# Decode attention over a 65,536-key cache: V loaded 8 MB at a time, and the first weight load in one piece

## The chip, the cores and the metric

The kernel runs on one core of a Trainium2 chip; the other cores are idle. The metric is device time in microseconds. The kernel before takes 1292.25 us (median of 3 runs, 1292.07 to 1292.52).

## What is computed

One token is decoded: layer norm, then attention with 16 query heads over 8 key/value heads, each with 65,536 cached keys and values of 256 bf16 elements, plus a small gated feed-forward part. The reference, cut to what matters:

```python
x  = A_x                                   # [1, 1, 448]
xn = _layernorm(x)
# attention: Hq = 16, Hkv = 8, Sk = 65536, Dh = 256, all bf16
q  = (xn @ wq)                             # wq: [448, 4096], 3.67 MB
k, v = repeat(k_cache, 2), repeat(v_cache, 2)   # each cache: 268 MB
p  = softmax(q k^T * Dh**-0.5)
a  = (p v) @ wo                            # wo: [4096, 448]
# the other part (w_gate, w_up, w_down: 448 x 1792 each, 1.6 MB)
y  = (silu(xn @ w_gate) * (xn @ w_up)) @ w_down * sigmoid(xn @ w_r)
out = x + a + xn + y
```

Nearly all of it is reading: K and V together are 537 MB, and every byte is used once (for the two query heads of its group).

## The kernel before

K and V go through a ring of 4 slots in SBUF. A slot is 128 partitions x 32 KB (4 MB): 64 keys or values of 256 bf16 for each partition. A head has 512 keys for each partition, so 4 turns (`U`) of 2 slots (`HC`).

```python
NSLOT = 4          # ring slots
CH = 64            # keys of one partition in a slot
HC = 2             # slots of K (or V) in a turn
LAST = [32, 16, 8, 8]
...
ring = S_("ring", [P, NSLOT * SLOT], BF16)          # SLOT = CH * Dh
```

All loads of the stream are issued by SyncE, in program order. A slot is filled again only when TensorE is through with the load that lay in it (`FREE`):

```python
def slot_item(kd, u, c, parts=None):
    src = A_k_cache if kd == "k" else A_v_cache
    h, n0 = u // U, (u % U) * SBN + c * CH
    r = rounds[0]
    rounds[0] += 1
    s = r % NSLOT
    ...
    for k, (sem, J) in enumerate(parts or [("slot%d" % s, CH)]):
        ap = ring[:, s * SLOT + o * Dh:s * SLOT + (o + J) * Dh]
        item((kd, u, c, k), [(ap.rearrange("p (j d) -> p j d", d=Dh),
                              src[0, h].rearrange("(p n) d -> p n d", p=P)[:, n0 + o:n0 + o + J, :], sem)],
             [("FREE", r - NSLOT)] if r >= NSLOT and k == 0 else ())
```

The order of the loads: wq in two parts; the K of the first head (8 slots, with the weights of the other part amid them); then 28 turns of K, V, V, K, in which the K are those of the next head; then 4 turns of V alone. The last slot of the ring is, in those 4 turns, cut in four parts (32, 16, 8 and 8 keys), so that TensorE can begin on it early.

```python
item("wq", [(w_area[o:e, 0:WQN], flat_src(A_wq, WQN)[o:e, :], "wq") for o, e in ((0, P // 8), (P // 8, P))])
for u in range(U):
    for c in range(HC):
        slot_item("k", u, c)
    if u == U // 2 - 1:
        item("wg", ...)      # w_gate, w_up: after the query is there
        item("wd_a", ...)
for t in range(NT):          # NT = 28
    slot_item("k", t + U, 0)
    slot_item("v", t, 0)
    slot_item("v", t, 1)
    if t % U == 0:
        item(("wo", t // U), ..., [("ATTN", t - 1)] if t else ())
    slot_item("k", t + U, 1)
for t in range(NT, NU):      # NU = 32
    for c in range(HC):
        slot_item("v", t, c, last_parts(rounds[0]) if rounds[0] % NSLOT == NSLOT - 1 else None)
```

`flat_src` views wq as 128 rows of 14,336 elements (28 KB), one for each partition.

TensorE's order in one of the 28 turns: it transposes and uses the first K slot (`k_slots`), multiplies the weights of the softmax with the first V slot (`pe_V`), sums the weights, uses the second V slot, then the second K slot. A V slot is waited for by its own semaphore and free when its last matmul is done:

```python
def turn_B(t):
    ...
    k_slots(sets_of(u, 0), s0, at)
    pe_V(t, 0, True, True)
    pe_tot(t)
    pe_V(t, 1, True, True)
    dve_ob(t)
    k_slots(sets_of(u, 1), s0, at)
    ...

def pe_V(t, c, first, last, loose=False):
    ...
    r, got = items[("v", t, c)]
    for k, (key, ap, o0, J) in enumerate(got):
        W_item("pe", key)
        ...
    alias("pe", "FREE", r)
```

At the end TensorE waits for the second half of w_down and for the last rows of wo, which are the last loads of the stream, and a short chain on TensorE and VectorE makes the result.

Of the kernel before, what the change touches and what calls it, by code (L numbers as in the profile page):

```python
# [11 lines left out]
NSLOT = 4  # L12
CH = 64
# [6 lines left out]
def bass_parallel_sum__gqa_block_cached__moe_arch_mod__decode_kernel(  # L20
# [17 lines left out]
    P = 128  # L38
    _, Hkv, Sk, Dh = A_k_cache.shape
# [16 lines left out]
    SBN = HC * CH  # L56
    SETS = SBN // SETN
    U = NPP // SBN
    NT = U * (Hkv - 1)
# [8 lines left out]
    SLOT = CH * Dh  # L68
    WQN, WGN, WDN, WON = RP * HqDh // 2, RP * F, FH * D, rep * NH * D
# [4 lines left out]
    def S_(name, shape, dtype):  # L74
        t = nc.sbuf_tensor(name, shape, dtype)
        sb.append(t)
        return t.__enter__()

    ring = S_("ring", [P, NSLOT * SLOT], BF16)
    w_area = S_("w_area", [P, WQN], BF16)  # L80
# [85 lines left out]
    def W(e, *key):  # L166
        prog[e].append(("w", here[0], key, None, None))
# [12 lines left out]
    items = {}  # L180
    semtot = {}
    rounds = [0]

    def item(key, parts, need=()):
        for n in need:
            W("sp", *n)
        for ap, src, sem in parts:
            semtot[sem] = semtot.get(sem, 0) + 16
            items[key] = (sem, semtot[sem])
            prog["sp"].append(("d", here[0], ("DMA", key, len(prog["sp"])), (ap, src), sem))  # L190

    def slot_item(kd, u, c, parts=None):
        src = A_k_cache if kd == "k" else A_v_cache
        h, n0 = u // U, (u % U) * SBN + c * CH
# [3 lines that stand above are left out]
        o = 0  # L198
        got = []
# [5 lines that stand above are left out]
            got.append(((kd, u, c, k), ap, o, J))  # L205
            o += J
        items[(kd, u, c)] = (r, got)

    def flat_src(src, n):
        return src.rearrange("a b -> (a b)").rearrange("(p n) -> p n", p=P)  # L210

    def wo_src(h):
        return A_wo[h * rep * Dh:(h + 1) * rep * Dh, :].rearrange("(i p f) n -> p i f n", i=rep, f=NH)

    def wo_view(t):
        return t.rearrange("p (i f n) -> p i f n", i=rep, f=NH)
# [4 lines left out]
    def last_parts(r):  # L221
        return [("last%d" % k if k < len(LAST) - 1 else "slot%d" % (r % NSLOT), J) for k, J in enumerate(LAST)]

    item("wq", [(w_area[o:e, 0:WQN], flat_src(A_wq, WQN)[o:e, :], "wq") for o, e in ((0, P // 8), (P // 8, P))])
    for u in range(U):
        for c in range(HC):
            slot_item("k", u, c)
        if u == U // 2 - 1:
            item("wg", [(w_area[:, 0:WGN // 2], flat_src(B_w_gate, F), "wg"),
                        (w_area[:, WGN // 2:WGN], flat_src(B_w_up, F), "wg")], [("QT",)])  # L230
            item("wd_a", [(wd_a[:, :], wd_src(0), "wd")])
    for t in range(NT):
        slot_item("k", t + U, 0)
        slot_item("v", t, 0)
        slot_item("v", t, 1)
        if t % U == 0:
            item(("wo", t // U), [(wo_view(wo_cur[:, :]), wo_src(t // U), "wo")], [("ATTN", t - 1)] if t else ())
        slot_item("k", t + U, 1)
    for t in range(NT, NU):
        for c in range(HC):  # L240
            slot_item("v", t, c, last_parts(rounds[0]) if rounds[0] % NSLOT == NSLOT - 1 else None)
    item("wd_b", [(w_area[:, 0:WDN], wd_src(1), "we0")], [("FFN1",)])
# [661 lines left out]
```

## Time and profile before

| | before |
|---|---|
| time, median of 3 | 1292.25 us |
| span of the profiled run | 1290.7 us |
| bytes moved | 549.22 MB, mean 426 GB/s |
| TensorE matmul busy | 926.4 us (72%) |
| VectorE busy | 586.1 us (45%) |
| ScalarE busy | 459.5 us (36%) |
| first K slot used by TensorE | 30.14 us |
| result leaves | 1289.19 us |

How to read the views: the page gives, for 40 equal slices of the span, the busy share of each engine in tenths and what the DMA engines moved in GB/s; a list of DMA issues with the size of each and the median time from issue to landing; and the chain that ended last, followed back from the last instruction. The timeline lists instructions in order of time: start and duration in us, engine, source line, operation, output<-input, count, and in brackets the idle time ahead of it and what ended it (`<-DMA ring` is a load into the ring). SPq is the queue of SyncE, which issues the loads; several issues with waits between them are merged in one line. In the table by stage, a line has the stretch, its length, the busy time of TensorE (matmuls, weight loads), VectorE, ScalarE and GpSimd with their counts, the clock granted to TensorE, the share of the 16 DMA engines that was busy, and GB/s; a packet's bytes are counted where it starts. A packet record is one descriptor's transfer by one DMA engine.

### The profile page before, as it was taken

Reading aid. Unit: us, or ns where it says so; the run is one execution under the profiler, and the core shown is the slowest. Engines: PE = TensorE matmul, PEld = TensorE weight load, DVE = VectorE, ACT = ScalarE, POOL = GpSimd, SP = SyncE. Lnnn points to the kernel's source line nnn. Section 1 sums busy time; section 2 is a strip of 40 time slices with the busy share of each in tenths; the row PEclk is TensorE's granted clock in tenths of the full one; section 3 lists DMA queues with packets and bytes.
Section 4 is the critical chain, followed back from the end, with each engine's and each line's share of the span. In section 5 each row is a group of like instructions: output and inputs, shape, how many; then the busy total and the mean of one; then the engine's idle time right before and its main releaser. Section 6 shows DMA issues by size and latency. Waiting matters only on the chain.

```text
span 1290.7 us, 22879 instructions
## 1 busy us (share of the span) xinstructions
PE 926.4 (72%) x9824; PEld 671.7 (52%) x9824; DVE 586.1 (45%) x1091; ACT 459.5 (36%) x655; POOL 4.6 (0%) x35
## 2 busy tenths in 40 slices
PE   1988776876767866768766668766678766678654
PEld 1867554654545654545645546545456544456421
DVE  2756444553445544445544445544345434455300
ACT  1545433442323533334433244333334333334300
POOL 1000000000000000000000000000000000000000
PEclk9989889988889888889878899888798888898876
DMA  9999999999999999999999999999999999999997
GB/s 307 423 434 434 429 432 433 428 437 429 432 434 429 435 431 432 433 431 434 431 432 432 431 434 431 433 432 431 434 430 434 432 430 435 430 434 432 430 431 317
DMA packets 22244, 549.22 MB, mean 426 GB/s; under 512 B 2387, under 2 KB 4438, under 8 KB 5206
## 3 DMA queue, kind: packets, MB, share of 16 engines
q1 hardware_dynamic: 22226, 549.04, 99.6%
q8 instruction: 8, 0.13, 0.0%
q14 instruction: 6, 0.05, 0.0%
q10 hardware_dynamic: 4, 0.00, 0.0%
HBM read 549.03 MB, written 0.00 MB: 425 GB/s over the span
## 4 chain that ended last, share of the span: by engine, by line
DMA 68%; PE 31%; SPq 0%; ACT 0%; issue 0%; DVE 0%
DMA ring<-in_A_k_cache_dram 63%; PE ps_t L352 24%; PE ps_q L352 5%; DMA w_area<-in_B_w_down_dram 3%; DMA ring<-in_A_v_cache_dram 2%; PE ps_s L352 1%; PE ps_m L352 1%; SPq L776 0%; ACT s L430 0%; DVE res_bf L727 0%; PE ps_o L352 0%
## 5 line engine op out<-in xcount | busy, mean ns | idle before, releaser
L352 PE MATMUL ps_t<-ident_f,ring 128*128 128x128 f32 x4096 | 568.7, 296 | 248.3 <-DMA ring<-in_A_k_cache_dram 229.2
L406 DVE COPY kt_buf<-ps_t 128x1024 bf16<-128x1024 bf16 x768 | 489.8, 683 | 427.0 <-PE ps_t L352 426.7
L352 PEld LDWEIGHTS ps_t<-ident_f,ring 128*128 128x128 f32 x4096 | 494.9, 152 | 354.3 <-DMA ring<-in_A_k_cache_dram 245.6
L408 ACT ACTIVATE kt_buf<-ps_t 128x1024 bf16<-128x1024 bf16 x256 | 262.1, 1024 | 357.9 <-PE ps_t L352 357.8
L430 ACT ACTIVATE s<-ps_q 98x512 bf16<-98x512 f32 x256 | 152.9, 597 | 288.0 <-PE ps_q L352 288.0
L352 PE MATMUL ps_o<-ring,p_sb 128*4 128x512 bf16 x2048 | 134.0, 404 | 67.5 <-DMA ring<-in_A_v_cache_dram 67.5
L352 PE MATMUL ps_q<-kt_buf,q_cur 128*2 128x512 bf16 x2048 | 166.4, 402 | 0.0
L352 PEld LDWEIGHTS ps_o<-ring,p_sb 128*4 128x4 bf16 x2048 | 48.0, 86 | 134.4 <-issue 77.6
L352 PEld LDWEIGHTS ps_s<-sel_bf,s 128*128 128x128 bf16 x1024 | 60.6, 99 | 54.1 <-ACT s L430 50.8
L540 DVE CAST ob_sb<-ps_o 100x512 bf16<-100x512 f32 x29 | 20.1, 692 | 144.5 <-PE ps_o L352 144.5
L352 PE MATMUL ps_s<-sel_bf,s 128*128 128x8 bf16 x1024 | 64.3, 168 | 22.6 <-ACT s L430 22.6
L497 ACT ACTIVATE p_sb<-S_sb 128x128 bf16<-128x128 bf16 x64 | 18.9, 307 | 136.1 <-PE ps_o L352 135.8
L576 DVE TENSOR_TENSOR rowsf<-ps_m,rowsf 1x448 f32<-1x448 f32 x28 | 17.1, 612 | 54.1 <-PE ps_m L352 54.1
L352 PEld LDWEIGHTS ps_q<-kt_buf,q_cur 128*2 128x2 bf16 x2048 | 27.1, 80 | 10.2 <-issue 5.0
L512 DVE RECIPROCAL rs<-ps_m 128x4 f32<-128x4 f32 x29 | 5.3, 182 | 52.8 <-PE ps_m L352 52.8
L352 PE MATMUL ps_m<-wo_cur,oT_sb 128*1 128x448 bf16 x112 | 25.8, 352 | 0.0
L352 PEld LDWEIGHTS ps_m<-rowsum,ones_f 128*128 128x128 f32 x116 | 15.1, 190 | 12.6 <-issue 12.6
L352 PE MATMUL ps_m<-rowsum,ones_f 128*128 128x2 f32 x116 | 17.6, 256 | 0.0
L352 PEld LDWEIGHTS ps_m<-wo_cur,oT_sb 128*1 128x1 bf16 x112 | 9.3, 83 | 13.6 <-issue 2.4
L454 DVE CAST S_sb<-ps_s 128x256 bf16<-128x256 f32 x32 | 12.9, 404 | 4.3 <-PE ps_s L352 4.3
L487 ACT ACTIVATE S_sb<-S_sb,negmax 128x512 bf16<-128x512 bf16 x16 | 13.4, 865 | 3.5 <-DVE negmax L481 3.5
L456 DVE TENSOR_REDUCE m1p<-S_sb 128x2 f32<-128x256 bf16 x32 | 13.5, 421 | 1.1
(79 smaller groups left out, 138.0 us busy)
## 6 DMA issues: line engine op xcount, KB each, us to landing
ring<-in_A_k_cache_dram SPq DMA_DIRECT2D x64, 4096.0 KB, 25.3
ring<-in_A_v_cache_dram SPq DMA_DIRECT2D x62, 4096.0 KB, 32.3
ring<-in_A_v_cache_dram SPq DMA_DIRECT2D x2, 2048.0 KB, 28.0
w_area<-in_A_wq_dram SPq DMA_DIRECT2D x1, 3136.0 KB, 18.3
wo_cur<-in_A_wo_dram SPq DMA_DIRECT2D x7, 448.0 KB, 15.6
ring<-in_A_v_cache_dram SPq DMA_DIRECT2D x2, 1024.0 KB, 30.1
ring<-in_A_v_cache_dram SPq DMA_DIRECT2D x4, 512.0 KB, 31.3
w_area<-in_B_w_gate_dram SPq DMA_DIRECT2D x1, 1568.0 KB, 40.2
```

Source lines behind the costliest of these rows:

```text
L352: return pe.matmul(*a, **k)
L406: O(e, ("EV", s, m), lambda it: nc.vector.tensor_copy(out=kt[:, :], in_=tb[:, :]), f"ev{m}")
L408: O(e, ("EV", s, m), lambda it: nc.scalar.activation(out=kt[:, :], in_=tb[:, :], func=ACTF.Copy), f"ev{m}")
L430: O("act", ("EVQ", s), lambda it: nc.scalar.activation(out=s2[s % 2][0:QROWS, :], in_=ps_q[0:QROWS, :], func=ACTF.Copy), "evq")
L454: O("dve", ("SCOPY", u), lambda it: nc.vector.tensor_copy(out=S, in_=ps_sn))
L456: O("dve", ("SMAX", u), lambda it: nc.vector.tensor_reduce(out=m1p[:, :, k], in_=S.rearrange("p n i -> p i n"), axis=AX.X, op=ALU.max))
L487: O("act", ("EXP", h, i), lambda it, i=i: nc.scalar.activation(out=S_sb[:, :, i], in_=S_sb[:, :, i], func=ACTF.Exp, bias=negmax[:, i:i + 1 ...
L497: O("act", ("PC", t, c), lambda it: nc.scalar.activation(out=p_sb[:, c, :, :], in_=S_sb[:, n:n + CH, :], func=ACTF.Copy), "pc")
L512: O("dve", ("RS", t), lambda it: nc.vector.reciprocal(out=rs[:, :, :], in_=ps_m[0:P, C_TOT:C_TOT + NH * rep]))
L540: O("dve", ("OB", t), lambda it: nc.vector.tensor_copy(out=ob_sb[0:OROWS, :], in_=ps_o[0:OROWS, :]))
L576: O("dve", ("RES", t), lambda it: nc.vector.tensor_tensor(out=base_f, in0=ps_m[0:1, C_BIG:C_BIG + D], in1=base_f, op=ALU.add))
```

## The change

There are two parts. V is loaded a turn at a time: one load of 8 MB fills two adjacent ring slots, and so each partition's 64 KB are one descriptor, where two loads had 32 KB each. It is for fewer loads and larger descriptors. The load waits until both slots are free, and both V slots of a turn are waited for by one semaphore. K, and the slots of the last turns that are cut in parts, stay as they were. In the second part the first load of the program, wq, is one load over 128 partitions instead of one over partitions 0 to 15 (a single descriptor for each of 16 DMA engines) and one over the other 112.

```diff
+    def pair_item(u):
+        h, n0 = u // U, (u % U) * SBN
+        r = rounds[0]
+        rounds[0] += 2
+        s = r % NSLOT
+        assert s + 1 < NSLOT
+        ap = ring[:, s * SLOT:(s + 2) * SLOT]
+        item(("v", u), [(ap.rearrange("p (j d) -> p j d", d=Dh),
+                         A_v_cache[0, h].rearrange("(p n) d -> p n d", p=P)[:, n0:n0 + 2 * CH, :], "slot%d" % s)],
+             [("FREE", r + i - NSLOT) for i in range(2)])
+        for c in range(2):
+            items[("v", u, c)] = (r + c, [(("v", u), ap[:, c * SLOT:(c + 1) * SLOT], 0, CH)])
...
-    item("wq", [(w_area[o:e, 0:WQN], flat_src(A_wq, WQN)[o:e, :], "wq") for o, e in ((0, P // 8), (P // 8, P))])
+    item("wq", [(w_area[:, 0:WQN], flat_src(A_wq, WQN), "wq")])
...
     for t in range(NT):
         slot_item("k", t + U, 0)
-        slot_item("v", t, 0)
-        slot_item("v", t, 1)
+        pair_item(t)
...
     for t in range(NT, NU):
+        if (t - NT) % 2 == 0:
+            pair_item(t)
+            continue
         for c in range(HC):
             slot_item("v", t, c, last_parts(rounds[0]) if rounds[0] % NSLOT == NSLOT - 1 else None)
```

## The prediction

> **What bounds the kernel now.** I read the page first: bandwidth by slice, the DMA queue and the chain that ended last.
>
> ```profile
> GB/s 307 423 434 434 429 432 433 428 437 429 432 434 429 435 431 432 433 431 434 431 432 432 431 434 431 433 432 431 434 430 434 432 430 435 430 434 432 430 431 317
> q1 hardware_dynamic: 22226, 549.04, 99.6%
> ...
> DMA 68%; PE 31%; SPq 0%; ACT 0%; issue 0%; DVE 0%
> ```
>
> The 16 DMA engines are busy for 99.6% of the span and move some 432 GB/s in every slice but the first two (307, 423) and the last (317). 549 MB at 432 GB/s are 1271 us of the 1290.7 us span. So the time is start of the stream + stream + tail, and the only places with something to win are the first 30 us, the small excess of each load, and the end. The second view is the table by stage.
>
> ```profile
> 1.76:6.40 4.64, 0.00 (x0) 0.00 (x0) 1.26 (x5) 1.04 (x1) 3.41 (x25) 1.00 1.18 198
> 6.40:19.50 13.10, 0.37 (x8) 0.28 (x8) 5.43 (x16) 1.85 (x6) 0.00 (x0) 1.00 0.98 268
> 19.50:30.10 10.60, 3.12 (x112) 3.07 (x112) 0.00 (x0) 0.40 (x2) 0.00 (x0) 1.00 0.99 422
> 30.10:78.40 48.30, 42.72 (x448) 34.55 (x448) 31.88 (x52) 25.55 (x32) 0.00 (x0) 0.96 1.00 429
> 160.00:1200.00 1040.00, 757.37 (x8078) 553.36 (x8076) 484.09 (x907) 375.80 (x534) 0.00 (x0) 0.89 1.00 432
> ```
>
> The last number is GB/s, the one before it the DMA share. Until 19.5 us the engines are busy (0.98 and more) but move 198 and 268 GB/s, half of what they do later. The issues tell what is in flight then: the two parts of wq.
>
> ```profile
> ring<-in_A_k_cache_dram SPq DMA_DIRECT2D x64, 4096.0 KB, 25.3
> ring<-in_A_v_cache_dram SPq DMA_DIRECT2D x62, 4096.0 KB, 32.3
> w_area<-in_A_wq_dram SPq DMA_DIRECT2D x1, 3136.0 KB, 18.3
> w_area<-in_A_wq_dram SPq DMA_DIRECT2D x1, 448.0 KB, 5.8
> ```
>
> 448 KB take 5.8 us to land and the other 3136 KB 18.3 us, though a 4 MB load of the stream takes 9.7 us (below). The K and V times are long only because each load is issued 2 to 3 loads ahead; that is the depth of the queue. The timeline of one turn shows the same.
>
> ```profile
> 474.12 13.36 SPq L776 DMA_DIRECT2D ring<-in_A_k_cache_dram  x2
> 487.58 1.90 PE L352 MATMUL ps_o<-ring,p_sb 128*4 128x512 bf16 x32
> 489.52 3.73 SPq L776 DMA_DIRECT2D ring<-in_A_v_cache_dram  x2
> 490.98 1.90 PE L352 MATMUL ps_o<-ring,p_sb 128*4 128x512 bf16 x32 [0.97 <-DMA ring<-in_A_v_cache_dram]
> 500.60 1.57 PEld L352 LDWEIGHTS ps_t<-ident_f,ring 128*128 128x128 f32 x8 [8.23 <-DMA ring<-in_A_k_cache_dram]
> ```
>
> TensorE uses the first V slot from 487.6 us, waits for the second until 491.0, is done with it at 492.9 and then waits for the next K until 500.6. Each V slot is filled again the moment it is free (489.5 and 492.9), while that K and another one are still ahead in the queue. Last, the loads at the end, which are cut in 4, 2, 1, 0.5 and 0.5 MB, with TensorE waiting for each:
>
> ```profile
> 1262.84 3.54 PE L352 MATMUL ps_o<-ring,p_sb 128*4 128x512 bf16 x32 [6.43 <-DMA ring<-in_A_v_cache_dram]
> 1272.55 3.58 PE L352 MATMUL ps_o<-ring,p_sb 128*4 128x512 bf16 x32 [6.17 <-DMA ring<-in_A_v_cache_dram]
> 1277.44 1.03 PE L352 MATMUL ps_o<-ring,p_sb 128*4 128x512 bf16 x16 [1.31 <-DMA ring<-in_A_v_cache_dram]
> 1279.85 1.02 PE L352 MATMUL ps_o<-ring,p_sb 128*4 128x512 bf16 x8 [1.36 <-DMA ring<-in_A_v_cache_dram]
> 1281.12 0.60 PE L352 MATMUL ps_o<-ring,p_sb 128*4 128x512 bf16 x4 [0.26 <-DMA ring<-in_A_v_cache_dram]
> 1282.40 0.60 PE L352 MATMUL ps_o<-ring,p_sb 128*4 128x512 bf16 x4 [0.68 <-DMA ring<-in_A_v_cache_dram]
> ```
>
> Each has the same 8 descriptors for each engine; only their size differs (32, 16, 8, 4, 4 KB).
>
> **What the Trainium skill says.** "SBUF — State Buffer", section "Door 1: The DMA port swizzle": partitions reach 16 ports, and 0 to 15 reach only 4 of them, 104 GB/s measured. The trace agrees: the packet records show the first part's 16 descriptors starting at 1.8 us and all landed by 6.5 us, 459 KB in 4.7 us or 98 GB/s. "DMA: Bandwidth & Descriptors", "Rules for kernel authors": two transfers to disjoint partition halves bring nothing, one of 128 partitions is to be used. The same page, "Where 436 GB/s comes from": the ceiling is 435.2 GB/s; the trace's 432 is 0.7% under it, so no descriptor size can bring more than 0.7% in mid-stream. The same page, "Why small descriptors are slow (HBM only)": a fixed overhead for each packet. The last loads agree: 4 MB take 1272.55 - 1262.84 = 9.71 us, 0.5 MB 1.275 us. With T = C + bytes x r, C = (8 x 1.275 - 9.71) / 7 = 0.07 us a load.
>
> **Part 1, the first load in one piece.** Removed: one issue (0.40 us of SyncE, in which nothing waits) and a load onto 16 partitions. Added: one load of 3.67 MB over all 128. The wq loads are the only ones in the kernel that don't cover 128 partitions, and the only slow ones. The packet records give a control: w_gate, as contiguous in HBM as wq but 128 partitions wide, has 12.25 KB descriptors of 469 ns each, 26.7 GB/s an engine, full rate. In the 112-partition part a 28 KB descriptor takes 1500 to 1950 ns, where 28672 B at 27.0 GB/s would be 1062. And the first K descriptors are at 1213 ns as soon as the last wq bytes have landed. So I take it that wq over 128 partitions runs at full rate: 8 descriptors x 1.062 = 8.5 us, from 1.8 us, or 2.0 as the descriptors for the last engines are made later than with a 16-descriptor load ahead. Done at 10.5, first K slot 9.71 later, 20.2; landing recorded some 0.4 later, 20.6. Now TensorE starts on it at 30.14: up to 9.5 us. From this I take off about 1 us, since one engine is delayed by an instruction fetch just then (one 32 KB packet of 1720 ns at 26.7 us) and may be again. The other way round: by 30.1 us the stream has moved 0.198 x 4.64 + 0.268 x 13.1 + 0.422 x 10.6 = 8.9 MB, which at 432 GB/s would take 20.6 us from 1.8, until 22.4: 7.7 us lost over all engines. Between 7.7 and 9.5, I take **8.4 us**.
>
> Does it reach the end? The stream is gapless from there to 1280 us, each issue follows a consumption that follows a landing, and nothing is tied to absolute time. The query must be ready before the first K slot: the layer norm's columns are in SBUF at 12.7 us, the projection takes 3.1 us, so 16 us is before 20.6. All 8.4 us are on the path.
>
> **Part 2, V in pairs.** 28 + 2 = 30 pairs take the place of 60 loads; 2 V loads of 4 MB and the cut ones stay. A pair has 8 descriptors of 64 KB for each engine instead of 16 of 32 KB. It saves one C: 0.07 by the fit above; by the cut load as a whole, 1282.40 - 1272.55 = 9.85 against 9.71 for three loads more, 0.05. So 30 x 0.06 = **1.8 us**, on the path since it is DMA time. TensorE loses its head start: the first V slot can only be used when the second has landed. At the turn above it would do both from 490.5 on, some 2 x 1.9 + 0.6 for the sums between, until about 495 instead of 492.9. The wait for K until 500.6 hides this. The pair goes out at 495 instead of 489.5 and 492.9; the DMA engines need it when this K and the next are through, 500.6 + 9.7 = 510: 15 us of reserve. In the last turns, where only V is left, a pair waits for one that landed two single loads earlier, minus 4.5 us: 15 us again.
>
> **Sum:** 1292.25 - 8.4 - 1.8 = 1282.05, so **1282 us** (-0.8%).
>
> **Rivals.** (a) The slow start is no matter of partitions but of a cold memory or of wq's place in HBM. Then the single load is as slow, only part 2 stays: 1290.5. For it: my port picture explains 98 GB/s in the first 4.7 us well, but not all of the following 268 GB/s. Also, someone made the split on purpose. Against it: the control of w_gate, and that the slowness ends with wq. I give it 15 to 20%. (b) The stream starves, because a pair needs two slots free at once: a new wait for DMA in front of each K. With 15 us of reserve it shouldn't; if half of the turns lost 2 us it would be +28 us, 1310. 3%. (c) 64 KB descriptors are cut in two or run slower. Cut in two, part 2 saves next to nothing (6 ns for the semaphore packet in the records): 1283.5. 15%. (d) Part 1 only half works, 11 us rather than 8.5 for wq: 1284.5.
>
> **Range and chances.** (c) and (d) lie within; below, the full 9.5 and 2.1 us with a better balanced end give 1280. Range **1279.5 to 1287**, which leaves out (a) and (b). Faster by over 2% would be under 1266: 0.01, since the start has no more than 9.5 us to give and the ceiling 0.7%. Slower by over 2% is over 1318: 0.01. Within 2%: 0.98.
>
> **What would show it.** Right: one wq issue that lands some 10 us after it; first K wait ended at 20 to 22 us; first slice near 400 GB/s; V issues x30 of 8192 KB; packets fewer by 30 x 144, the 16 semaphore packets included; the V wait one for each pair, K waits shorter by some 2 us each turn, but none gone. Step wrong if: the first K still starts near 30 us (a), turns take over 38.85 us from K to K (b, c), or the packet count falls by only 30 x 16 (c). The prediction as a whole fails if the stream shows slices under 428 GB/s in its middle.

## The result, and the profile after

The changed kernel takes 1283.03 us (median of 4, 1282.19 to 1283.18) against 1292.35 us: ratio 0.9927, 95% interval 0.991 to 0.9944. The predicted time was 1282, the range 1279.5 to 1287.

The page of the changed kernel, the same lines as of before: GB/s by slice, the queue of the loads (packets, MB, share), the chain by engine.

```profile
GB/s 406 424 436 424 450 426 427 431 431 439 436 438 417 437 430 441 432 430 428 432 446 426 436 424 436 430 444 430 428 428 433 441 436 430 425 435 431 434 437 310
...
q1 hardware_dynamic: 17890, 549.04, 99.5%
...
DMA 69%; PE 30%; SPq 0%; ACT 0%; issue 0%; DVE 0%
```

It is still bound by the DMA engines. The first slice rose from 307 to 406 GB/s. The packets fell by 22226 - 17890 = 4336: 30 pairs x 144, and 16 semaphore packets of the wq load that is gone. So the 64 KB descriptors are real; in the packet records 3840 packets of 65,536 bytes take 2422 ns each in the mean. The slices in the middle now scatter from 417 to 450, since a 64 KB packet is counted where it starts: with each packet's bytes spread over the time it took, the slices between the second and the last but one read 428 to 433. The table by stage has no such scatter.

```profile
1.76:6.40 4.64, 0.00 (x0) 0.00 (x0) 1.25 (x4) 1.05 (x1) 3.40 (x25) 1.00 1.09 396
6.40:19.50 13.10, 3.52 (x120) 3.35 (x120) 5.46 (x16) 2.26 (x8) 0.00 (x0) 1.00 1.00 430
19.50:30.10 10.60, 7.31 (x51) 6.70 (x52) 4.07 (x7) 3.17 (x4) 0.00 (x0) 1.00 1.00 431
30.10:78.40 48.30, 42.74 (x453) 34.59 (x452) 32.15 (x53) 25.81 (x33) 0.00 (x0) 0.93 1.00 430
160.00:1200.00 1040.00, 803.44 (x8047) 549.22 (x8046) 479.93 (x900) 373.95 (x532) 0.00 (x0) 0.86 1.00 432
```

Where 198 and 268 GB/s were moved at the start, it is now 396 and 430. The timeline of the start shows what comes of it. In the kernel before, the query's matmuls wait for wq:

```profile
19.66 3.12 PE L352 MATMUL ps_m<-xnT_sb,w_area 128*128 128x2 bf16 x112 [8.39 <-DMA w_area<-in_A_wq_dram]
30.14 5.57 PE L352 MATMUL ps_t<-ident_f,ring 128*128 128x128 f32 x32 [7.36 <-DMA ring<-in_A_k_cache_dram]
```

Now they no longer do, and the first K slot is used at 22.79 us instead of 30.14, 7.35 us sooner.

```profile
13.90 3.15 PE L367 MATMUL ps_m<-xnT_sb,w_area 128*128 128x2 bf16 x112 [1.63 <-ACT xnT_sb L355]
22.79 5.59 PE L367 MATMUL ps_t<-ident_f,ring 128*128 128x128 f32 x32 [5.74 <-DMA ring<-in_A_k_cache_dram]
```

Two turns of the timeline show the pair at work: both V slots are used one after the other once the pair has landed (482.73 and 521.51), then the next pair is issued, then K is waited for.

```profile
482.73 3.58 PE L367 MATMUL ps_o<-ring,p_sb 128*4 128x512 bf16 x32 [4.25 <-DMA ring<-in_A_v_cache_dram]
487.18 3.58 PE L367 MATMUL ps_o<-ring,p_sb 128*4 128x512 bf16 x32
490.86 0.33 SPq L791 DMA_DIRECT2D ring<-in_A_v_cache_dram  x1
492.35 1.97 PE L367 MATMUL ps_t<-ident_f,ring 128*128 128x128 f32 x16 [1.58 <-DMA ring<-in_A_k_cache_dram]
...
521.51 3.58 PE L367 MATMUL ps_o<-ring,p_sb 128*4 128x512 bf16 x32 [5.79 <-DMA ring<-in_A_v_cache_dram]
525.55 1.90 PE L367 MATMUL ps_o<-ring,p_sb 128*4 128x512 bf16 x32
527.54 0.33 SPq L791 DMA_DIRECT2D ring<-in_A_v_cache_dram  x1
531.13 3.04 PE L367 MATMUL ps_t<-ident_f,ring 128*128 128x128 f32 x16 [3.68 <-DMA ring<-in_A_k_cache_dram]
```

After the wait of 4 to 6 us the same 32 matmuls take 3.58 us instead of 1.90, sometimes for both slots. The Trainium skill, "TensorE: Matmul & The Clock Gate", Part 1, tells of a clock at half rate until TensorE has been busy for about 3.4 us. The trace agrees in kind: the granted clock reads 0.50 over both V slots of the first turn, and in the second 0.51 over the first slot and 1.00 over the next. It does not agree in length: in the first turn the slow stretch lasts the whole 8 us. It costs nothing here, since K comes later still. The waits of TensorE for the ring (sum in us, times, longest), in the kernel before and in the changed one:

```profile
PE ps_t L352 <- DMA ring<-in_A_k_cache_dram: 229.2, 30, 8.8
...
PE ps_o L352 <- DMA ring<-in_A_v_cache_dram: 67.5, 37, 9.4
```

```profile
PE ps_o L367 <- DMA ring<-in_A_v_cache_dram: 148.3, 36, 19.1
...
PE ps_t L367 <- DMA ring<-in_A_k_cache_dram: 99.1, 30, 6.8
```

### The profile page after: what moved, and what is told of

It is laid out like the page before. It is cut to its first block, busy times and chain, and to the rows that moved or that the text cites. A ratio compares the mean times of both kernels' runs of the same rounds, so it can differ in the third digit from the quotient of the medians.

```text
span 1281.2 us, 22851 instructions
## 1 busy us (share of the span) xinstructions
PE 971.8 (76%) x9824; PEld 668.1 (52%) x9824; DVE 584.6 (46%) x1091; ACT 459.4 (36%) x655; POOL 4.5 (0%) x35
## 3 DMA queue, kind: packets, MB, share of 16 engines
q1 hardware_dynamic: 17890, 549.04, 99.5%
## 4 chain that ended last, share of the span: by engine, by line
DMA 69%; PE 30%; SPq 0%; ACT 0%; issue 0%; DVE 0%
DMA ring<-in_A_k_cache_dram 64%; PE ps_t L367 23%; PE ps_q L367 5%; DMA w_area<-in_B_w_down_dram 3%; DMA ring<-in_A_v_cache_dram 2%; PE ps_s L367 1%; PE ps_m L367 1%; SPq L791 0%; ACT s L445 0%; DVE res_bf L742 0%; PE ps_o L367 0%
## 5 line engine op out<-in xcount | busy, mean ns | idle before, releaser
L367 PE MATMUL ps_t<-ident_f,ring 128*128 128x128 f32 x4096 | 551.1, 290 | 118.1 <-DMA ring<-in_A_k_cache_dram 99.1
L367 PEld LDWEIGHTS ps_t<-ident_f,ring 128*128 128x128 f32 x4096 | 478.4, 148 | 225.4 <-DMA ring<-in_A_k_cache_dram 118.5
L367 PE MATMUL ps_o<-ring,p_sb 128*4 128x512 bf16 x2048 | 189.5, 533 | 148.4 <-DMA ring<-in_A_v_cache_dram 148.3
L367 PEld LDWEIGHTS ps_o<-ring,p_sb 128*4 128x4 bf16 x2048 | 55.3, 104 | 253.9 <-issue 228.5
L367 PEld LDWEIGHTS ps_m<-rowsum,ones_f 128*128 128x128 f32 x116 | 21.6, 262 | 22.3 <-issue 22.3
L367 PE MATMUL ps_m<-rowsum,ones_f 128*128 128x2 f32 x116 | 24.0, 312 | 0.0
```

What stands on the lines that cost most here:

```text
L367: return pe.matmul(*a, **k)
```

## Experiments

Times are medians, the ratio is to the kernel before run beside them.

| run | wq | V | ring | time us | ratio (95%) |
|---|---|---|---|---|---|
| changed kernel | one load | pairs | as it was | 1283.03 | 0.9927 (0.991 to 0.9944) |
| e1 | one load | single | as it was | 1284.91 | 0.9941 (0.9927 to 0.9954) |
| e2 | 16 + 112 | pairs | as it was | 1290.04 | 0.9981 (0.9973 to 0.9988) |
| e3 | one load | two loads, issued and awaited as a pair | as it was | 1285.22 | 0.9943 (0.9929 to 0.9956) |
| e4 | one load | pairs, 32 KB descriptors | 128 B between slots | 1281.72 | 0.9916 (0.9903 to 0.993) |
| e5 | cut along the rows | pairs | as it was | 1282.53 | 0.9926 (0.9912 to 0.994) |
| e6 | 64 + 64 | pairs | as it was | 1292.22 | 0.9998 (0.999 to 1.0007) |
| e7 | one load; w_gate, w_up 16 + 112 | pairs | as it was | 1291.39 | 0.9993 (0.9986 to 0.9999) |
| e8 | one load | single | 128 B between slots | 1280.90 | 0.9911 (0.9896 to 0.9927) |
| e9 | one load | pairs | 128 B, not in the long part's pairs | 1281.22 | 0.9911 (0.9896 to 0.9926) |
| e10 | one load | pairs | 512 B behind the ring | 1282.61 | 0.9923 (0.991 to 0.9937) |
| e11 | one load | single | 128 B further on | 1280.56 | 0.9911 (0.9897 to 0.9924) |
| e12 | one load | pairs | 128 B further on | 1279.54 | 0.9903 (0.9887 to 0.9918) |

**e1 and e2: each part alone.** e1 is the kernel before with one line changed, e2 the changed kernel with that line put back:

```diff
-item("wq", [(w_area[o:e, 0:WQN], flat_src(A_wq, WQN)[o:e, :], "wq") for o, e in ((0, P // 8), (P // 8, P))])
+item("wq", [(w_area[:, 0:WQN], flat_src(A_wq, WQN), "wq")])
```

> The kernel before with part 1 alone: wq as one load over 128 partitions, V still in loads of 4 MB. Theory (the two parts add up, the first slot of K comes 7.35 us sooner as in the changed kernel): 1292.3 - 7.3 = 1285.0 us, first K slot used at 22.8 us, turns of 38.85 us from K to K. Rival (the gain is mostly of the pairs): 1290 us or more.

> The kernel before with part 2 alone: V in pairs, wq still in two loads. Theory (0.07 us for each of 30 pairs): 1292.3 - 2.1 = 1290.2 us, first K slot used at 30.1 us, turns of 38.78 us. Rival (waiting for both halves costs what the larger descriptors save): 1292.3 us.

e1 is 7.65 us faster than the kernel before, e2 2.5 us, their sum 10.2 where both parts together gave 9.3. The single times of a run scatter by about 1 us and medians of the kernel before differ by 0.3 us from one set to another, so nothing is read from the 0.9 us between. The first K slot is used at 22.72 us in e1 and at 29.69 us in e2. Both rivals fall: three quarters or more of the gain are the start, and the pairs do save something.

**e5: two loads at the start, all partitions.**

```diff
-item("wq", [(w_area[:, 0:WQN], flat_src(A_wq, WQN), "wq")])
+item("wq", [(w_area[:, o:e], flat_src(A_wq, WQN)[:, o:e], "wq") for o, e in ((0, WQN // 8), (WQN // 8, WQN))])
```

> The changed kernel with wq in two loads again, but cut along the rows: 3.5 KB, then 24.5 KB of each of the 128 partitions. Two loads of the same sizes as in the kernel before, each over all partitions. Theory (what was slow is the span of partitions, not that there were two loads): 1283.0 us, first K slot used at 22.8 us. Rival (two loads at the start are slow): 1290 us, 30 us.

1282.53 us: as fast as one load. Its two loads have the sizes of the kernel before, 448 and 3136 KB. That there were two was not the matter.

**e6: two loads over half of the partitions each.**

```diff
+item("wq", [(w_area[o:e, 0:WQN], flat_src(A_wq, WQN)[o:e, :], "wq") for o, e in ((0, P // 2), (P // 2, P))])
```

> The changed kernel with wq in two loads over partitions 0 to 63 and 64 to 127. Theory (each half reaches 8 of 16 ports, so 217 GB/s for all of wq): 3.67 MB take 16.9 us instead of 8.4, wq landed at 20 us, first K slot used at 31 us, 1291.3 us. Rival (the odd count of 112 partitions, or of 16, is what is slow): 1283.1 us.

1292.22 us, 9.2 us more than the changed kernel: all that part 1 gains is lost. The first K slot is used at 32.22 us, and both this and the time are about 1 us later than expected. The table by stage of this run:

```profile
1.76:6.40 4.64, 0.00 (x0) 0.00 (x0) 1.24 (x4) 1.04 (x1) 3.38 (x25) 1.00 1.11 241
6.40:19.50 13.10, 0.37 (x8) 0.29 (x8) 5.46 (x16) 1.85 (x6) 0.00 (x0) 1.00 0.97 202
19.50:30.10 10.60, 3.12 (x112) 3.07 (x112) 0.00 (x0) 0.40 (x2) 0.00 (x0) 1.00 1.01 419
```

The theory rests on what the Trainium skill states in "SBUF — State Buffer", "Door 1: The DMA port swizzle": partitions 0 to 63 reach no more ports than 0 to 31, half of them; 217 GB/s is an estimate, by the 218 or so that the page gives for 8 ports. The trace agrees to within 7%: wq's packets run from 2.1 to 20.3 us, 202 GB/s over all (the 241 of the first line counts packets where they start), and the median 28 KB descriptor takes 2236 ns where the changed kernel's takes 1062. The DMA share reads 0.97 and more all the while: busy engines are no sign of a full rate.

**e7: the same cut in mid-stream.** w_gate and w_up are loaded at about 50 to 60 us; here each is cut in partitions 0 to 15 and the rest.

```diff
+item("wg", [(w_area[o:e, f * (WGN // 2):(f + 1) * (WGN // 2)], flat_src(src, WGN // 2)[o:e, :], "wg")
+            for f, src in enumerate((B_w_gate, B_w_up)) for o, e in ((0, P // 8), (P // 8, P))], [("QT",)])
```

> The changed kernel with w_gate and w_up, which are loaded amid the stream at 50 to 60 us, each cut as wq was in the kernel before: partitions 0 to 15, then the other 112. Theory (the span of partitions is slow at any time, 98 GB/s and 268 GB/s as at the start): 0.2 MB at 98 instead of 432 GB/s and 1.4 MB at 268 instead of 432, each of the two +1.6 +2.0 us, 7.2 us together: 1290.2 us. Rival (the start is slow because it is the start): 1283.1 us.

1291.39 us, 8.4 more than the changed kernel (7.2 expected). The stretch in the changed kernel, and twice as long in this one:

```profile
49.30:59.40 10.10, 10.10 (x113) 8.15 (x113) 8.18 (x15) 6.34 (x9) 0.00 (x0) 1.00 0.99 415
```

```profile
49.30:69.30 20.00, 16.19 (x184) 12.50 (x182) 13.07 (x23) 10.68 (x14) 0.00 (x0) 0.96 1.00 221
```

The start has no part in it: cut into 16 and 112 partitions, a load runs at half the rate here too. With e5 and e6 this shows part 1's cause, the span of partitions that a load covers. That the ports are the reason is the page's account; it fits the 202 GB/s of 64 partitions and, roughly, the 98 of 16. Why 112 partitions run at only 268 GB/s is open.

**e3: the waits of a pair, with single loads.**

```diff
-item(("v", u), [(ap.rearrange("p (j d) -> p j d", d=Dh),
-      A_v_cache[0, h]...[:, n0:n0 + 2 * CH, :], "slot%d" % s)], ...)
+item(("v", u), [(ap[:, c * SLOT:(c + 1) * SLOT].rearrange("p (j d) -> p j d", d=Dh),
+      A_v_cache[0, h]...[:, n0 + c * CH:n0 + (c + 1) * CH, :], "slot%d" % s) for c in range(2)], ...)
```

> The changed kernel, but a pair is made as two loads of 4 MB with 32 KB descriptors, issued together when both slots are free, and both waited for before the first V slot is used. All waits as in the changed kernel, only the loads as before. Theory (the gain of part 2 is in the load itself, and the lost head start costs nothing): 1283.0 + 2.1 = 1285.1 us. Rival (the gain comes from when V is issued or waited for): 1283.0 us; rival (the head start is worth something that the larger load hides): over 1286 us.

1285.22 us, as e1 (1284.91): the later issue and the lost head start of TensorE cost nothing, and the gain of part 2 (2.2 us from here to the changed kernel) lies in the load itself.

**e4: one load, but 32 KB descriptors.** The gap breaks each partition's 64 KB in two.

```diff
+SG = SLOT + 64                                   # distance of slots, 128 bytes more
-ap = ring[:, s * SLOT:(s + 2) * SLOT]
+ap = ring[:, s * SG:(s + 2) * SG]                # written as [p, 2, SLOT]
```

> The changed kernel with 128 bytes left free between ring slots, so that a pair is still one load of 8 MB, but each partition's part is two descriptors of 32 KB. Tells the number of descriptors from the number of loads. Theory (about 8.5 ns for each descriptor, 6 ns for the semaphore packet of a load): 8 descriptors more an engine and pair, 30 x 8 x 8.5 ns = 2.0 us more, 1285.0 us. Rival (a fixed cost of each load): 1283.0 us.

1281.72 us: faster than either theory allows, with all 16,128 packets at 32 KB. By itself it decides nothing, since the gap moved something else as well. The packet records give a hint: without gaps a 32 KB packet mostly takes 1213, 1218 or 1221 ns, in the mean 1216.9 in e1; with them 1213 in nearly 9 of 10 cases.

**e8, e9, e10: the gap by itself, the gap with 64 KB descriptors, and the padding alone.**

```diff
# e8: e1 with SG = SLOT + 64 as the distance of slots
# e9: changed kernel with slots at
+OFF = [0, SLOT + 64, 2 * SLOT + 64, 3 * SLOT + 128]
# e10: changed kernel with
+ring = S_("ring", [P, NSLOT * SLOT + 256], BF16)
```

> No pairs: the kernel before with wq as one load, and 128 bytes left free between ring slots. The run with pairs and the gap came out faster than the changed kernel though it has 32 KB descriptors, and its packets took 1213 ns nearly all where the others mix 1213, 1218 and 1221. Theory (the gap itself takes some 3 ns off each descriptor): turns of 38.76 us, 1284.9 - 3 = 1282 us. Rival (it is the one load for each pair that does it): 1284.9 us, turns of 38.86 us.

> The changed kernel with 128 bytes free between slots 0 and 1 and between 2 and 3, but none between 1 and 2, so that the 28 pairs of the long part keep one 64 KB descriptor for each partition. Theory (the two savings, 3 ns of each descriptor by the gap and 8 descriptors of 8.5 ns by the pairs, add up): 1281.7 - 28 x 8 x 8.5 ns = 1279.8 us. Rival (the gap must lie inside the pair to help): 1283 us.

> The changed kernel with 512 bytes added behind the ring: the slots stay where they are, everything allocated after the ring moves as far as in the run with gaps. Theory (the place of the slots against each other matters): 1283.0 us. Rival (it is where the other tensors lie): 1281 us.

e8, without any pair, takes 1280.90 us, 4.0 less than e1 and less than the changed kernel. e10 leaves the time where it was (1282.61), so it is where the slots lie, not where the other tensors do. e9 (1281.22) missed its 1279.8, and the landings of its loads say why: a pair takes 19.30 us where the changed kernel's takes 19.35, but a K load takes 9.71 as it does without gaps. Here K lies at 0 and 256 bytes from its old place, and only the pairs, at 128, gain. And e4 against e8 is the clean comparison that e4 was meant to be: same gaps, same descriptors, one load for each pair instead of two, and no gain (1281.72 against 1280.90; by the landings 19.38 us for the pair and 9.66 + 9.71 = 19.37 for its two loads). So what a pair saves is descriptors, not loads.

**e11 and e12: the whole ring 128 bytes further on,** without and with pairs.

```diff
+lead = S_("lead", [P, 64], BF16)
 ring = S_("ring", [P, NSLOT * SLOT], BF16)
```

> No pairs, no gaps: the kernel before with wq as one load, and the whole ring 128 bytes further on. In the runs with gaps a 4 MB load into a slot 128 or 384 bytes off took 9.66 us, and one into a slot 0 or 256 bytes off 9.71, like all loads of the kernels without a gap. Theory (it is the start address of each descriptor in SBUF, odd multiples of 128 bytes from where the ring was being faster by 57 ns a load): turns of 38.63 us, 128 loads x 0.057 = 7.3 us less than with the single wq load alone, 1284.9 - 7.3 = 1277.6 us. Rival (the slots' distance from each other is what counts): 1284.9 us.

> The changed kernel with the whole ring 128 bytes further on. Tells what the pairs are worth where the start address costs nothing: a pair there took 19.29 us (with gaps outside the pair), two single loads 2 x 9.657 = 19.31. Theory (most of what pairs save is that half as many descriptors start at a slow address): 30 x 0.02 = 0.6 us under the same without pairs, 1277 us. Rival (pairs save 0.07 us each whatever the address): 2.1 us under it, 1275.5 us.

The chain of e11 and then of e12, in order of time (start and duration of the wait for a K load; start + duration is the landing):

```profile
464.87 26.63 DMA ring<-in_A_k_cache_dram
...
503.06 27.16 DMA ring<-in_A_k_cache_dram
...
541.30 27.65 DMA ring<-in_A_k_cache_dram
```

```profile
464.74 26.09 DMA ring<-in_A_k_cache_dram
...
500.60 28.91 DMA ring<-in_A_k_cache_dram
...
540.86 27.33 DMA ring<-in_A_k_cache_dram
```

The landings in e11 are at 491.50, 530.22 and 568.95: turns of 38.72 us; in e12 at 490.83, 529.51 and 568.19: 38.68. For comparison the kernel before and then the changed kernel:

```profile
474.12 26.44 DMA ring<-in_A_k_cache_dram
...
512.38 27.03 DMA ring<-in_A_k_cache_dram
...
550.69 27.58 DMA ring<-in_A_k_cache_dram
```

```profile
464.84 27.47 DMA ring<-in_A_k_cache_dram
...
502.08 29.01 DMA ring<-in_A_k_cache_dram
...
542.38 27.50 DMA ring<-in_A_k_cache_dram
```

Turns of 38.85 and 38.78. So no gap is needed: the slots' distances in e11 are the old ones, and it is the start address in SBUF that matters; the rival falls. The size was wrong: 1280.56 us, 4.35 less than e1, where 7.3 were expected. I had read two speeds of slots out of e8 (landings 9.656, 9.715, 9.658 and 9.713 us apart); in e11, where all slots should have been fast, all loads take 9.68, the mean of the two. The direction of the rule "odd multiples of 128 bytes" holds in every run with moved slots, e4 and e9 too, where loads into slots at 0 or 256 bytes took 9.71 as before; its size does not, 0.03 us for each 4 MB load in e11. In the program as built the ring starts at byte 16512 of each partition, 128 past a multiple of 256, and in e11 and e12 at 16640, a multiple of 256. So the faster slots are those that start at a multiple of 256 bytes. In e12 the pairs bring 1.0 us, nearer to the 0.6 than to the 2.1 expected: about half of what they save at the old address (1284.91 - 1283.03 = 1.9) is saved by the 128 bytes as well. e12, at 1279.54 us, beats both kernels.

Why such a start is faster was not found. In e8 the packets take 1213 ns in the slower slots as well, so the time of a packet does not tell. Only moves by 128, 256 and 384 bytes were run.

## Why the prediction was right

**The bound** and the place of the gain were right: DMA throughout, most of it in the first 30 us, and every us won at the start arrives at the end. The last loads of the stream have landed by 1275.71 us in the changed kernel and 1285.27 us before, 9.56 us apart, of which 7.35 were there at the first K slot.

**Part 1, mechanism right, size 8.4, measured 7.35.** The term that was mis-sized is the start of the single load. I took all eight descriptors at 1062 ns; the records show that for most of the last seven, but the first on each engine takes 1471 to 2293 ns, 0.75 us too much in the mean. wq has landed at 11.2 to 12.1 us, the first K slot at 21.3 in the median engine instead of 20.6, and in the slowest at 22.74: the delay beside an instruction fetch, for which I took off 1 us, was 1.5. The kernel before has this delay too (28.49 in the median engine, 30.10 in the slowest), so it belonged on both sides of the comparison. The prediction's other estimate, 7.7 us from the bytes moved by 30.1 us, was the nearer one. The rival of a cold start, given 15 to 20%, is refuted by e5 and e7 as the cause of the slow wq; the first descriptors, 0.75 us, are all that could be left of it. That the ports give 98 GB/s for the first part of wq was read too closely: this counts to its landings at 6.5 us, while its packets end by 5.2 us, which is 131 GB/s. The total of 1282 is 1 us under the measured 1283.03 because part 1 gave 1 us less than reckoned.

**Part 2, size nearly right for a reason that was half right.** 1.8 us predicted; 1.9 between e1 and the changed kernel, 2.2 between e3 and it, and 38.85 - 38.78 = 0.07 in each turn. But the constant C of 0.07 us, which I put down to each load, belongs to its descriptors (e4 against e8), and not as a fixed price: the shift by 128 bytes takes 0.03 of it from a 4 MB load. In e8 the loads of 0.5 MB at the end, which go to a faster slot, are 1.224 us apart in the median engine, where they were 1.27 to 1.29. One load less saves little beside that: the semaphore packet at its end takes 9 ns in the records.

**The reserve.** No turn starves, as predicted. I put TensorE's work on a pair at 4.4 us; it takes 6 to 8, because of the slow matmuls. The prediction's own lines of the last loads showed them, 3.54 and 3.58 us for 32 after waits of 6 us. So K waits became shorter by (229.2 - 99.1) / 30 = 4.3 us a turn rather than 2, and the pair issued at 490.86 has a reserve of 492.3 + 9.7 - 490.9 = 11 us rather than 15. Enough, but a third less than reckoned.

**A bad test.** I wrote that the prediction would fail if slices in mid-stream fell under 428 GB/s. They do (417), without meaning, for the reason given at the page above.

## What to carry to other kernels

A load that covers only some of the partitions can run at two thirds of the rate or far less (268 GB/s on 112, 202 on halves, 98 on 16, against some 430) while the DMA engines read as fully busy; look at GB/s by stage, not at their share, and cut a first load along the rows if it is to be cut at all. Where a stream has no gaps, what is left is in nanoseconds for each descriptor, and a gain from larger descriptors should be tried against moving the buffer, here to a multiple of 256 bytes, before its waits are accepted. When an engine loses its head start, reckon its work at its slow pace, not at the pace it had without the wait.

## What was not expected of the hardware

- Moving the ring by 128 bytes, from byte 16512 to 16640 of each partition, takes 0.03 us off each 4 MB load (9.714 to 9.68), 4.35 us off the whole kernel, 0.34%: more than twice what the pairs bring at the old address (1.9 us).
- The first descriptor of the program's first large load takes 1.5 to 2.3 us on each DMA engine in the changed kernel, where later ones of the same 28 KB take 1.06.
- After waits of 4 to 6 us, TensorE runs the V matmuls at a granted clock of 0.50, 3.58 us for 32 instead of 1.90, for 4 to 8 us.
